# Attention with a token mixer on one core: values on 64 rows of keys, eight tiles and two banks of sums, two banks of scores

## The chip, the cores and the metric

The kernel runs on one core of one Trainium2 chip. Its metric is the device time of one execution in microseconds (us). TensorE (PE) multiplies, VectorE (DVE), ScalarE (ACT) and GpSimd (POOL) do the rest, SyncE (SP) issues most DMAs. PE's results go to PSUM, which has eight banks of 128 x 512 float32; DVE and ACT read them there.

## The reference

`x` is 2048 x 512, `xn` its layer norm. Two branches start from `xn`, and their product is added to `x`:

```
qkv = xn @ wqkv                      # 32 heads of 16
p   = softmax(q @ k.T / 4)           # per head, 2048 x 2048
s   = (p @ v) @ wo
h   = layernorm(xn)
u   = gelu(h.T @ w1 + b1)            # over tokens: 512 x 1792
g   = silu((u @ w2 + b2).T)          # 2048 x 512
out = x + s * g
```

## The kernel before

**Stages.** First come the layer norms and the projections: q and k are written to DRAM in two float32r parts (upper and lower), v as it is. Then a long loop does the attention and, between its matmuls, the mixer branch. At the end the output projection is completed.

**The long loop.** Two heads make a pair; there are 16 pairs. The variable `s` goes by twos. For each pair there is a pass of maxima (`max_of`, line 387: q rows against keys, and on VectorE a maximum of each row, line 391, tile `mxp`) and, `LEAD` = 20 units later, a pass of scores (`score`, line 757, tile `sc`) whose exponentials ScalarE writes to `prob` (line 762). `values` (line 773) multiplies `prob` by `vp`, which holds the values of the pair with a column of ones for the denominator, and sums over the 16 blocks of 128 keys into the bank `av`. A call of `values` is four matmuls, one for each head of the pair and half of the queries; each has all 128 rows of the array and 32 columns, at the output partitions 32j to 32j + 31. They are float32, and each gives two weight loads and two matmuls in the profile. There are 512 calls. After 16 of them `put_away` (line 509) copies the bank to SBUF with ScalarE and sends it to DRAM; for the last pair `own` keeps it on the chip.

**Halves.** Maxima and scores contract over 48 and 50 rows. The heads of a pair sit in partitions 0 to 63 and 64 to 127, so a matmul of one head uses one half of the array's rows, and two matmuls, one in each half, run side by side. The mixer's matmuls (fillers, "D", line 911 after `halves`, tile `dn`) are cut into two of 64 rows for the same reason.

**Order.** The kernel schedules by hand: every engine gets its instructions in the order of the Python code. Within a step of two units, `ORDERS` says which kinds stand in which slot, for the two halves: `s` a score, `m` a maximum, `D` a filler. For six fillers:

```
6: ("DDDDDDsmsmsmsm", "msmsmsmsDDDDDD", 7),
```

`values` of one unit is called ahead of the slot with the number at the end (7), and of the other unit at the end of the step. `run_later` runs what was put off with `after` and `later`.

**Banks of PSUM.** A tile of a pool waits until the last reader of the tile that had its bank is done:

```
ps_sc = pool("ps_sc", 3, space=PSUM)
ps_mx = pool("ps_mx", 3, space=PSUM)
ps_av = pool("ps_av", 1, space=PSUM)
ps_dn = pool("ps_dn", 1, space=PSUM)
```

`ps_sc` holds scores, `ps_mx` maxima, `ps_av` the sums of the values, `ps_dn` those of the mixer and of the output projection. In the projections `bank()` deals out all eight in turn. For `s` below 20, maxima of the second half use `ps_sc` too. From `s` = 512 on there are no more maxima, and the scores of the second half use `ps_mx`. At that time `take` puts whole 128-row fillers (line 886) behind the values.

Of the kernel before, what the change touches and what calls it, by code (L numbers as in the profile page):

```python
# [8 lines left out]
F32 = mybir.dt.float32  # L9
F32R = mybir.dt.float32r  # L10
AF = mybir.ActivationFunctionType
OP = mybir.AluOpType
AX = mybir.AxisListType
PSUM = bass.MemoryType.PSUM
# [7 lines left out]
def tile_attention_token_mixer(ctx, tc, x, wqkv, wo, w1, b1, w2, b2, out):  # L22
    nc = tc.nc
    P = 128
# [5 lines left out]
    NB = S // P  # L30
    ND = D // P
# [9 lines left out]
    def pool(name, bufs, **kw):  # L41
        return ctx.enter_context(tc.tile_pool(name=name, bufs=bufs, **kw))
# [3 lines left out]
    big = pool("big", 4)  # L46
    wp = pool("wp", 4)
    dram = pool("dram", 1, space=DRAM)
    ps_sc = pool("ps_sc", 3, space=PSUM)
    ps_mx = pool("ps_mx", 3, space=PSUM)  # L50
    ps_av = pool("ps_av", 1, space=PSUM)
    ps_dn = pool("ps_dn", 1, space=PSUM)
    ctx.enter_context(tc.manual_schedule())

# [20 lines left out]
    def sub(eng, o, a, b):  # L75
        eng.tensor_tensor(out=o, in0=a, in1=b.bitcast(F32), op=OP.subtract)  # L76

    def move(dst, src, queue=nc.sync):

        queue.dma_start(dst.bitcast(F32), src.bitcast(F32))  # L80
# [7 lines left out]
    qs, ks, vps = {}, {}, {}  # L88
# [62 lines left out]
    with (  # L151
# [26 lines left out]
        for part in range(3):  # L178
            for kd in range(ND):
                nm = ("raw", "wh", "wl")[(part * ND + kd) % 3]  # L180
# [69 lines left out]
        def bank():  # L250

            i = turn_of[0] = (turn_of[0] + 1) % 8
            pl, nm = ((ps_sc, "sc"), (ps_mx, "mx"), (ps_dn, "dn"), (ps_av, "av"))[i % 2 if i < 6 else i - 4]
            return pl.tile([P, 512], F32, name=nm)

        for f in first(0).pieces():
# [14 lines left out]
        for c in range(NC):  # L271
# [23 lines left out]
            for n, (part, g) in enumerate(order):  # L295
                m = slice(g * P, (g + 1) * P)
                ps = bank()
                for w, z in ((wh, 0), (wh, 1), (wl, 0)):
                    for kd in range(ND):
                        nc.tensor.matmul(  # L300
                            ps, w[part][:, kd, m], xt[kd][:, z, :],
                            start=w is wh and z == 0 and kd == 0, stop=w is wl and kd == ND - 1,
# [63 lines left out]
    def after(n, f):  # L366

        later.append(f if n == 1 else lambda: after(n - 1, f))
# [140 lines left out]
    def put_away(p, span, av):  # L509

        ev = el.tile([P, 512], F32, name="ev")
        nc.scalar.copy(ev, av)
        if p == NP - 1:
            own(span, ev)
            return
        g, i = divmod(p, 4)
        if i == 0:
            dens[span] = sm.tile([P, 64], F32, name="d")
        rows = ev.rearrange("(j r) q -> r j q", r=32)
        for a in range(2):  # L520
            h = 2 * i + a
            nc.sync.dma_start(
                dens[span][DH * h : DH * (h + 1), :],
                rows[16 - 16 * a, 2 * a : 2 * a + 2, :].rearrange("c (j q) -> c j q", q=64),
            )
        nc.sync.dma_start(num_d[g][span][160 * i : 160 * i + P, :], ev)
        if i == 3 or p == NP - 2:
            invert(g, span)

    def heads_of(g):  # L530

        return 8 if g < ND - 1 else 6

    def invert(g, span):

        n = heads_of(g)
        d = dens[span][: DH * n, :]

        def two():
            nc.vector.reciprocal(d, d)  # L540
            nc.sync.dma_start(rec_d[g][span][:n, :].rearrange("h (j q) -> (h j) q", j=16), d)
            away.add((g, span))

        after(8 if g < ND - 1 else 4, two)
# [3 lines left out]
    divided = set()  # L548
# [52 lines left out]


    asides = []
    own_done = [False]

    def own(span, ev):
        rq = sm.tile([P, 4, 4], F32, name="rq", bufs=1)
        wide = el.tile([P, 512], F32, name="t", bufs=4)

        def one(pl=ps_mx, nm="mx"):  # L610

            ps = pl.tile([P, 512], F32, name=nm)
            for k in range(4):
                at = slice(k * P, (k + 1) * P)
                nc.tensor.transpose(ps[:, at], ev[:, at], ident)
            turned = ps.rearrange("p (k j r) -> p k j r", k=4, j=4)
            for a in range(2):
                nc.vector.reciprocal(rq[:, :, 2 * a : 2 * a + 2], turned[:, :, 2 * a : 2 * a + 2, 16 - 16 * a])
            nc.vector.tensor_copy(
                wide.rearrange("p (k j r) -> p k j r", k=4, j=4), rq.unsqueeze(3).to_broadcast([P, 4, 4, 32]),  # L620
            )

        def two(pl=ps_mx, nm="mx"):

            ps = pl.tile([P, 512], F32, name=nm)
            for k in range(4):
                nc.tensor.matmul(
                    ps[:, k * P : (k + 1) * P], wide[:, k * P : (k + 1) * P], ident, start=True, stop=True,
                )
            return ps  # L630

        def chunk(ps, of, at):
            nc.vector.tensor_tensor(out=ev[:, at], in0=ps[:, at], in1=ev[:, at], op=OP.mult)
            nc.scalar.copy(of[:, 0, at], ev[:, at])
            sub(nc.vector, of[:, 1, at], ev[:, at], of[:, 0, at])

        if span == QH - 1:
            asides.extend((one, two, chunk))
            return

        def move_in():
            ps = two()
            of = el.tile([P, 2, 512], F32R, name="uo")
            chunk(ps, of, slice(0, 512))
            for a in range(2):
                for c in range(2):
                    row = 32 * (2 * a + c) + DH * a
                    move(oc[ND - 1, c][96 + DH * a : 112 + DH * a, :, :], of[row : row + DH, :, :], nc.gpsimd)
            own_done[0] = True

        asides.extend((one, move_in))


# [93 lines left out]
    state = {}  # L747
    prob = {}
# [15 lines left out]
    def values(t):  # L764
        p, r = divmod(t, SPP)
        span, kb = divmod(r, NB)
        if kb == 0:
            state["av"] = ps_av.tile([P, 512], F32, name="av")
        av = state["av"]
        for a in range(2):  # L770
            for c in range(2):
                j = 2 * a + c
                nc.tensor.matmul(  # L773
                    av[32 * j : 32 * j + 32, :],
                    vps[p][:, kb, 16 * a : 16 * a + 32], prob.pop((t, a, c)),
                    start=kb == 0, stop=kb == NB - 1,
                )
        if kb == NB - 1:
            later.append(lambda: put_away(p, span, av))

    def rest():

        for n in range(N_W - 2, N_W):
            w_split(n)
        for b in range(2):
            load_part(b)

        def until(ready):
            while not ready():
                yield None  # L790

        def products(ps, b, groups, rows=None):
            at = slice(b % 4 * P, (b % 4 + 1) * P)
            for g in groups:
                o = oc[g, b // 4]
                at_g = rows if g == ND - 1 else None
                for j, (m, w) in enumerate(((0, whs), (0, wls), (1, whs))):
                    w = w[N_MIX + g].rearrange("p a b -> p (a b)")
                    yield (
                        ps, lambda r, o=o, m=m, s=at_g: o[s or r, m, at], lambda r, w=w, s=at_g: w[s or r, :],  # L800
                        g == groups[0] and j == 0, g == groups[-1] and j == 2,
                    )

        for b in range(PARTS):
            yield from until(lambda: all((g, b // (NB // QH)) in divided for g in range(ND - 1)))
            ps = ps_dn.tile([P, 512], F32, name="dn")[:, :D]
            yield from products(ps, b, range(ND - 1))
            yield lambda b=b, ps=ps: part(b, ps)
            yield None
        load_last_w()  # L810
        yield from until(lambda: now[0] >= NU and (ND - 1, QH - 1) in divided)
        for n in range(4):
            load_out(n)
        for n, b in enumerate(blocks):
            if n == NB // 2:
                yield from until(lambda: own_done[0] and (ND - 1, 0) in divided)
            ps = ps_dn.tile([P, 512], F32, name="dn")[:, :D]
            rows = slice(0, DH * heads_of(ND - 1) if n < NB // 2 else P)
            if b >= PARTS:
                yield from products(ps, b, range(ND), rows)  # L820
            else:
                yield from products(ps, b, [ND - 1], rows)
            yield lambda n=n, ps=ps: finish(n, ps)
            yield None

    def everything():
        yield from mixer()
        yield from rest()
# [115 lines left out]
    for s in range(0, total + 1, 2):  # L944
        t = s - LEAD
# [79 lines left out]
        if 0 <= t < NT:  # L1025
            p, r = divmod(t, SPP)
# [18 lines left out]
        take(3, lambda x, f: left.append(f) if f else whole(x, f))  # L1045
    for f in left:
        f()
    banks = [(ps_sc, "sc"), (ps_mx, "mx"), (ps_sc, "sc"), (ps_mx, "mx"), (ps_sc, "sc"), (ps_av, "av"), (ps_mx, "mx"), (ps_dn, "dn")]
    half = [NB // 2 + 4 * c + k for k in range(4) for c in range(2)]
    for n, b in enumerate(half):  # L1050
        pl, nm = banks[n]
# [37 lines left out]
```

## Time and profile before

| | us |
|---|---|
| median of 3 runs | 1708.33 (1707.89 to 1708.73) |
| the profiled execution | 1709.11 |
| its span | 1707.3 |
| PE busy | 1672.8 (98%) |
| DVE busy | 1409.7 (83%) |
| ACT busy | 1187.9 (70%) |
| POOL busy | 567.1 (33%) |

The span is the time from the first to the last instruction of that execution. Lines of the page read: line of the kernel, engine, operation, output <- input, shapes and count, then busy time in us and the mean of one in ns, then idle time of the engine just before them and what ended it. "PEld" is a weight load. Shapes such as `128*32` are rows x columns of the array that a matmul uses. In the timeline the columns are start and length in us. The granted clock of TensorE was 0.995 of full speed over the span. The first maximum starts at 153 us, the first score at 207 us, the last maximum at 1613 us and the last score at 1685 us.

### The profile page before, as it was taken

How to read it: one execution, taken by the hardware profiler on the slowest of the kernel's cores; microseconds unless marked ns; L12 is line 12 of the kernel's file. 1: busy time of each engine (PE TensorE's matmuls, PEld its weight loads, DVE VectorE, ACT ScalarE, POOL GpSimd, SP SyncE). 2: the span in 40 equal slices, each digit the busy share in tenths (PEclk: the TensorE clock that was granted, in tenths of full speed). 3: DMA queues.
4: the chain of work that ended last, by engine and by line, in shares of the span. 5: the costliest groups of instructions: out<-in, count | busy, mean ns of one | idle time of the engine just before them, and what ended most of it. 6: DMA issues, size and time to landing. Idle time of an engine off the chain costs nothing.

```text
span 1707.3 us, 30652 instructions
## 1 busy us (share of the span) xinstructions
PE 1672.8 (98%) x11716; PEld 846.9 (50%) x11716; DVE 1409.7 (83%) x2378; ACT 1187.9 (70%) x2291; POOL 567.1 (33%) x673
## 2 busy tenths in 40 slices
PE   7999999999999999999999999999999999999987
PEld 6887644444444444444444444444444444444443
DVE  6565888888888888888888888888888888888834
ACT  3333277777777777777777777777777777787845
POOL 4223842233342334333422322222222222463401
PEclk9999999999999999999999999999999999999999
DMA  6467611415150514353332415141515132272435
GB/s 222 179 235 184 133 44 42 75 44 85 45 85 20 92 46 68 135 127 94 75 60 64 79 35 82 36 80 31 81 33 82 37 48 52 78 158 85 147 98 186
DMA packets 150879, 152.94 MB, mean 90 GB/s; under 512 B 51452, under 2 KB 109820, under 8 KB 147660
## 3 DMA queue, kind: packets, MB, share of 16 engines
q1 hardware_dynamic: 146188, 149.97, 36.8%
q0 software_dynamic: 4544, 1.01, 0.4%
q8 instruction: 92, 1.51, 0.4%
q14 instruction: 55, 0.45, 0.1%
HBM read 100.29 MB, written 49.53 MB: 88 GB/s over the span
## 4 chain that ended last, share of the span: by engine, by line
PE 92%; DVE 5%; ACT 1%; DMA 0%; issue 0%; POOL 0%; SPq 0%; DVEq 0%; POOLq 0%
PE av L773 28%; PE dn L911 26%; PE mx L387 13%; PE sc L757 12%; DVE mxp L391 4%; PE dn L886 3%; PE mx L300 2%; PE sc L300 2%; ACT prob L762 1%; PE av L886 1%; PE av L300 1%; PE dn L300 1%; PE mx L757 1%; PE mx L402 0%; PE sc L83 0%
## 5 line engine op out<-in xcount | busy, mean ns | idle before, releaser
L391 DVE TENSOR_REDUCE mxp<-mx 128x1 f32<-128x512 f32 x2008 | 1250.5, 683 | 183.9 <-PE mx L387 97.4
L762 ACT ACTIVATE prob<-sc 128x512 f32<-128x512 f32 x2008 | 1041.8, 604 | 331.1 <-PE sc L757 252.6
L387 PE MATMUL mx<-big 48*128 48x512 f32 x2008 | 826.8, 428 | 2.1
L757 PE MATMUL sc<-big 50*128 50x512 f32 x2008 | 771.8, 428 | 3.4 <-DMA big<-m 2.0
L911 PE MATMUL dn<-hu,wh 64*128 64x512 f32 x1570 | 573.8, 406 | 0.0
L773 PE MATMUL av<-prob,vp 128*32 128x512 f32 x4096 | 546.3, 605 | 0.0
L387 PEld LDWEIGHTS mx<-big 48*128 48x128 f32 x2008 | 364.2, 186 | 221.8 <-DVE mxp L391 206.6
L757 PEld LDWEIGHTS sc<-big 50*128 50x128 f32 x2008 | 355.1, 185 | 191.7 <-ACT prob L762 173.3
L911 PEld LDWEIGHTS dn<-hu,wh 64*128 64x128 f32 x1570 | 289.3, 185 | 171.5 <-issue 145.5
L911 PE MATMUL dn<-hu,wl 64*128 64x512 f32 x786 | 316.3, 402 | 0.0
L145 POOL CAST wh<-raw 128x512 fp32r<-128x512 f32 x108 | 62.8, 582 | 327.3 <-PE dn L911 309.6
L76 POOL TENSOR_TENSOR wl<-raw,wh 128x512 fp32r<-128x512 f32 x124 | 150.3, 1215 | 38.6 <-ACT wh L147 29.9
L773 PEld LDWEIGHTS av<-prob,vp 128*32 128x32 f32 x4096 | 81.0, 108 | 150.6 <-issue 138.6
L911 PEld LDWEIGHTS dn<-hu,wl 64*128 64x128 f32 x786 | 145.9, 186 | 8.3 <-issue 0.8
L406 POOL CAST m<-f 16x128 fp32r<-16x128 f32 x32 | 9.0, 280 | 266.1 <-DVE f L405 266.1
L464 POOL TENSOR_TENSOR sq<-u 128x512 f32<-128x512 f32 x14 | 14.6, 1040 | 170.9 <-ACT u L463 170.9
L80 POOL DMA_DIRECT2D big<-m x128 | 67.7, 535 | 0.0
L762 ACT ACTIVATE prob<-mx 128x512 f32<-128x512 f32 x40 | 25.1, 627 | 29.2 <-PE sc L757 22.0
L500 POOL TENSOR_SCALAR t<-t 128x512 f32<-128x512 f32 x16 | 23.8, 1488 | 62.4 <-ACT t L497 62.4
L911 PE MATMUL dn<-wh,hu 64*128 64x512 f32 x120 | 41.6, 399 | 0.0
L76 POOL TENSOR_TENSOR hu<-hx,hu 128x512 fp32r<-128x512 f32 x16 | 20.4, 1291 | 54.6 <-ACT hu L243 54.6
L300 PE MATMUL mx<-xt,big 128*128 128x512 f32 x144 | 35.4, 395 | 0.0
(202 smaller groups left out, 1094.2 us busy)
## 6 DMA issues: line engine op xcount, KB each, us to landing
raw<-in_B_w_dram SPq DMA_DIRECT2D x104, 256.0 KB
big<-k_d SPq DMA_DIRECT2D x96, 128.0 KB
big<-q_d SPq DMA_DIRECT2D x96, 128.0 KB
q_d<-sg SPq DMA_DIRECT2D x16, 512.0 KB
k_d<-sg SPq DMA_DIRECT2D x16, 512.0 KB
num_d<-ev SPq DMA_DIRECT2D x30, 256.0 KB
u_d<-uo SPq DMA_DIRECT2D x14, 512.0 KB
hu<-u_d SPq DMA_DIRECT2D x14, 512.0 KB
```

The costliest lines, as they stand in the source:

```text
L76: eng.tensor_tensor(out=o, in0=a, in1=b.bitcast(F32), op=OP.subtract)
L80: queue.dma_start(dst.bitcast(F32), src.bitcast(F32))
L145: nc.gpsimd.tensor_copy(whs[n][:, :m, :], raws[n][:, :m, :])
L300: nc.tensor.matmul(ps, w[part][:, kd, m], xt[kd][:, z, :], start=w is wh and z == 0 and kd == 0, stop=w is wl and kd == ND - 1,)
L387: nc.tensor.matmul(ps, q[o : o + 48, r * P : (r + 1) * P], k[o : o + 48, c * 512 : (c + 1) * 512], start=True, stop=True,)
L391: nc.vector.tensor_reduce(mxp[u // 16][:, a, r % 8, c : c + 1], ps, axis=AX.X, op=OP.max)
L500: nc.gpsimd.tensor_scalar(t, t, 1.0, None, op0=OP.add)
L757: nc.tensor.matmul(ps, ks[p][o : o + 50, kb * P : (kb + 1) * P], qs[p][o : o + 50, at : at + 512], start=True, stop=True,)
L762: nc.scalar.activation(e, ps, AF.Exp, scale=scale)
L773: nc.tensor.matmul(av[32 * j : 32 * j + 32, :], vps[p][:, kb, 16 * a : 16 * a + 32], prob.pop((t, a, c)), start=kb == 0, stop=kb == NB - 1,)
L886: nc.tensor.matmul(ps, w(slice(0, P)), m(slice(0, P)), start=first, stop=last)
L911: made.append(lambda r=r, start=first and a == lead, stop=last and a != lead: nc.tensor.matmul(ps, w(r), m(r), start=start, stop=stop,))
```

## The change

- `values` makes eight matmuls of 64 rows of keys by 32 columns in place of four of 128 rows by 32 columns. Rows 0 to 63 sum into one bank, rows 64 to 127 into a second one.
- `put_away` copies the first bank with ScalarE and adds the second to it with VectorE.
- `ps_av` gets two banks, and `ps_sc` two in place of three.
- The turns of `bank()` and the list of output banks at the end follow the new numbers of banks. `own_done` is set two runs of `run_later` later.

```diff
-    ps_sc = pool("ps_sc", 3, space=PSUM)
+    ps_sc = pool("ps_sc", 2, space=PSUM)
     ps_mx = pool("ps_mx", 3, space=PSUM)
-    ps_av = pool("ps_av", 1, space=PSUM)
+    ps_av = pool("ps_av", 2, space=PSUM)
...
-            pl, nm = ((ps_sc, "sc"), (ps_mx, "mx"), (ps_dn, "dn"), (ps_av, "av"))[i % 2 if i < 6 else i - 4]
+            pl, nm = ((ps_sc, "sc"), (ps_mx, "mx"), (ps_av, "av"), (ps_dn, "dn"))[(0, 1, 2, 1, 0, 1, 2, 3)[i]]
...
         ev = el.tile([P, 512], F32, name="ev")
-        nc.scalar.copy(ev, av)
+        nc.scalar.copy(ev, av[0])
+        nc.vector.tensor_tensor(out=ev, in0=av[1], in1=ev, op=OP.add)
...
-    own_done = [False]
+    own_done = []
...
-            own_done[0] = True
+            after(2, lambda: own_done.append(True))
...
-            state["av"] = ps_av.tile([P, 512], F32, name="av")
+            state["av"] = [ps_av.tile([P, 512], F32, name="av") for _ in range(2)]
         av = state["av"]
         for a in range(2):
             for c in range(2):
                 j = 2 * a + c
-                nc.tensor.matmul(
-                    av[32 * j : 32 * j + 32, :],
-                    vps[p][:, kb, 16 * a : 16 * a + 32], prob.pop((t, a, c)),
-                    start=kb == 0, stop=kb == NB - 1,
-                )
+                e = prob.pop((t, a, c))
+                for half in range(2):
+                    rows = slice(64 * half, 64 * half + 64)
+                    nc.tensor.matmul(
+                        av[half][32 * j : 32 * j + 32, :],
+                        vps[p][rows, kb, 16 * a : 16 * a + 32], e[rows, :],
+                        start=kb == 0, stop=kb == NB - 1,
+                    )
...
-                yield from until(lambda: own_done[0] and (ND - 1, 0) in divided)
+                yield from until(lambda: own_done and (ND - 1, 0) in divided)
...
-    banks = [(ps_sc, "sc"), (ps_mx, "mx"), (ps_sc, "sc"), (ps_mx, "mx"), (ps_sc, "sc"), (ps_av, "av"), (ps_mx, "mx"), (ps_dn, "dn")]
+    banks = [(ps_sc, "sc"), (ps_mx, "mx"), (ps_sc, "sc"), (ps_mx, "mx"), (ps_av, "av"), (ps_av, "av"), (ps_mx, "mx"), (ps_dn, "dn")]
```

## The prediction

> **What bounds the kernel now.** The page comes first. Its parts 1 and 5 say that TensorE is never off for long, and which matmuls fill it:
>
> ```profile
> PE 1672.8 (98%) x11716; PEld 846.9 (50%) x11716; DVE 1409.7 (83%) x2378; ACT 1187.9 (70%) x2291; POOL 567.1 (33%) x673
> ...
> L762 ACT ACTIVATE prob<-sc 128x512 f32<-128x512 f32 x2008 | 1041.8, 604 | 331.1 <-PE sc L757 252.6
> ...
> L773 PE MATMUL av<-prob,vp 128*32 128x512 f32 x4096 | 546.3, 605 | 0.0
> ```
>
> The value products (line 773) have 4096 records, eight to a call, so 512 calls at 546.3 / 512 = 1.07 us. A busy PE hides its stalls, since a matmul's end is modelled. The weight loads show them, so the list of waits is next:
>
> ```profile
> PEld mx L387 <- DVE mxp L391: 206.6, 300, 0.8
> PEld sc L757 <- ACT prob L762: 173.3, 495, 1.1
> ```
>
> Already with three banks of scores a score's weight load is held 495 times until ScalarE has emptied a bank. How such a wait sits in a step is seen in the timeline of one step of two rows of scores (PE, then the loads, then ScalarE: one exponential alone, and the four from the same start merged):
>
> ```profile
> 705.99 1.07 PE L773 MATMUL av<-prob,vp 128*32 128x512 f32 x8
> ...
> 708.54 0.40 PE L387 MATMUL mx<-big 48*128 48x512 f32 x1
> 708.87 1.06 PE L773 MATMUL av<-prob,vp 128*32 128x512 f32 x8
> 709.87 0.49 PE L911 MATMUL dn<-hu,wh 64*128 64x512 f32 x1
> 709.87 0.49 PE L387 MATMUL mx<-big 48*128 48x512 f32 x1
> 710.20 0.39 PE L911 MATMUL dn<-hu,wl 64*128 64x512 f32 x1
> 710.21 0.40 PE L757 MATMUL sc<-big 50*128 50x512 f32 x1
> 710.43 0.39 PE L911 MATMUL dn<-hu,wh 64*128 64x512 f32 x1
> ```
>
> ```profile
> 705.56 0.18 PEld L757 LDWEIGHTS sc<-big 50*128 50x128 f32 x1 [0.20 <-ACT prob L762]
> ...
> 711.74 0.16 PEld L773 LDWEIGHTS av<-prob,vp 128*32 128x32 f32 x8 [0.24 <-issue]
> ```
>
> ```profile
> 704.91 0.60 ACT L762 ACTIVATE prob<-sc 128x512 f32<-128x512 f32 x1 [0.94 <-PE sc L757]
> ...
> 704.91 2.06 ACT L762 ACTIVATE prob<-sc 128x512 f32<-128x512 f32 x4 [0.94 <-PE sc L757]
> ```
>
> What to read. Two matmuls, one in each half of the rows, make a slot of 0.23 us (710.20 to 710.43). Between two calls of the values lie seven slots, and a step is two such windows: from the values at 705.99 to those at 711.74, 5.75 us. A call stretches its place: from the last slot before it (708.54) to the next pair (709.87) are 1.33 us, and that pair then runs 0.49 in place of 0.39 because its weights were not loaded ahead, 0.10 more. So last slot to effective next slot is 1.43, and a window is 7 x 0.23 + 1.43 - 0.23 = 2.81.
>
> A bank of scores is taken for a cycle that the lines give piece by piece. The matmul runs 0.40; ScalarE starts 0.06 later (a score that began at 704.45 ends at 704.85, its exponential starts at 704.91); this takes 0.60; the waiting load begins 0.05 after it (705.51 to 705.56); the load costs 0.10. Sum 1.21 us. ScalarE works faster than that when it has a queue: four in 2.06, so (2.06 - 0.60) / 3 = 0.49 apart.
>
> By the order in the code (the six-filler row of ORDERS), counting slots of a window from 0, the scores stand in slots 1, 3, 5, 6 ahead of the middle values and in 0, 1, 3, 5 behind them. Three banks: in the first window the score of slot 6 (1.38) needs the bank of slot 1 (0.23 + 1.21 = 1.44), 0.06 late; in the second the score of slot 5 (1.15) needs that of slot 0 (1.21), 0.06 late. Step: 2 x 2.81 + 0.12 = 5.74 against 5.75 in the trace. The reading holds, and it can be done again with two banks.
>
> **The change part by part.**
>
> *Two banks of scores.* First window: scores at 0.23 and 0.69; the third (1.15) waits for the first's bank until 1.44, 0.29 late. The second's exponential starts at max(0.69 + 0.46, 0.69 + 0.49) = 1.18 and ends at 1.78, so its bank serves the fourth at 1.93 in place of 1.67, 0.26 more. Together 0.55, against 0.06 now. While the values run, ScalarE empties both banks. Second window: scores at 0 and 0.23; the third (0.69) waits until 1.21, 0.52 late; the second's exponential runs 0.95 to 1.55, bank at 1.70, 0.03 more. Together 0.55 against 0.06. TensorE takes its matmuls in order, so what stands behind the held score (the maxima for VectorE and the fillers of the other half) is held too, and nothing covers it. Per step 2 x 0.49 = 0.98. There are 246 steps that hold both maxima and scores (s from 20 to 510, by twos). 246 x 0.98 = 241 us. If the release were 20% quicker or slower than these rows, 190 to 290.
>
> *Ten steps of the tail* put half the scores on these banks, three in adjacent slots ahead of the values: the third waits from 0.46 to 1.21, 0.75. Some 8 us.
>
> *The first twenty rows of maxima* use the score banks for half of their maxima: five banks in place of six, beside a VectorE that is busy 9.88 of 10.00 us there. TensorE only queues deeper. I take 4, between 0 and 10.
>
> *Values in eight tiles.* The work per row of the array is unchanged: twice the instructions, each on half the rows, all eight at once. The nearest row for halves is the slot itself, whose two 64-row matmuls start within 0.01 us (710.20, 710.21); that for narrow tiles is the present call, whose eight loads take 0.16 us where one takes 0.108, so (0.16 - 0.108) / 7 = 7 ns from one to the next. Four more loads ahead of the last first pass: 4 x 7 = 28 ns, x 512 = 14 us. The bounds are -164 us (all 0.32 of the stretch of a call, 1.43 - 0.23 - 0.88, gone; 0.88 is a call's own streaming, two passes, the second of which starts 0.45 behind the first, at 706.44, and streams 0.43) and +450 (halves one after the other, 0.88 x 512). I take +14, since all rows around are slots in which halves run together. The Trainium skill, "TensorE: Matmul & The Clock Gate", Part 3, puts an additional tile at about 4 ns; by that figure the 14 us would be an estimated 8. No run yet shows eight tiles.
>
> *Two banks of sums, added on put_away.* 32 times VectorE gets one more pass over 128x512 from the sum bank, about the 0.68 of a maximum (it starts one per 0.60), after ScalarE's copy (0.59). The next call that needs these banks begins a window later, 2.81 + 0.55 = 3.36 after the last one, which itself takes 1.06: 2.30 are left, and three hand-overs of 0.06, the copy, up to 0.60 of a running maximum and 0.68 make 2.05. Cover gone, it costs up to 32 x 1.3 = 40. VectorE stands idle some 0.4 us in each 2.87 us window, which takes the added pass. I take 4.
>
> *Rotations of banks in the projections, own_done two calls later, last output bank:* eight banks in eight turns before and after; the delay falls once. Nothing.
>
> Sum against the profiled execution's own 1709.1 us (span 1707.3 and 1.8 around it; the median of the runs is 1708.33): 1709.1 + 241 + 8 + 4 + 14 + 4 = 1980.
>
> **The rivals.**
>
> *A. The switch between tile shapes gets cheap, because the array stays at 64 rows.* The rows speak against it. Ahead of the tail's fillers only the width of the tile changes, with 128 rows kept:
>
> ```profile
> 1625.47 1.07 PE L773 MATMUL av<-prob,vp 128*32 128x512 f32 x8
> 1626.47 0.50 PE L886 MATMUL dn<-wh,hu 128*128 128x512 f32 x1
> ...
> 1629.12 0.39 PE L886 MATMUL dn<-wh,hu 96*128 96x512 f32 x1
> 1629.43 0.50 PE L757 MATMUL mx<-big 50*128 50x512 f32 x1
> ```
>
> From the call to the next matmul 1.00 us, as from 708.87 to 709.87 where rows and width both change; and where only the rows change, 0.31 for a slot of 0.23 and an exposed load again. Any change of shape pays. For A: no row has 64 rows by 32 columns. It would take 0.11 ahead of the call and 0.10 behind it away, 0.21 x 512 = 107: 1873 us, and 1816 if the load is hidden as well. The Trainium skill, "TensorEngine Tiling (Array Packing)", Key Properties, says that a change of tiling mode drains TensorE; by that rule A saves nothing, and the tail's rows agree. Chance 14%.
>
> *B. Faster: the values take half the time.* If each half of the rows streamed its own share at double speed and no switch were left, a call would be 0.45 in place of 1.20 beyond its slot: -0.75 x 512 = -384, so 1596. It decides for faster from 271 / 512 = 0.53 us saved per call. Against it: matmuls of 48, 50 and 64 rows hold a slot of 0.23 exactly as those of 128 rows do (1626.81 to 1627.04), so fewer rows buy no speed. Chance 5%.
>
> *C. The halves run one after the other*, +450 on the sum without the 14: 2416. Against it the pairs of each slot. Chance 5%.
>
> *D. The lost bank binds nothing.* Then only the small terms stay: 1709 + 22 to 30, about 1735. Against it the 495 waits with three banks and a reading that gives the step to 0.01 us. Chance 3%.
>
> **How the numbers follow.** Forecast 73%, time 1980. Its own range, from 190 to 290 for the banks and 0 to 40 for the sums, is 1925 to 2060. The range takes in A's 1873: 1860 to 2060, leaving out B, C, D and the far end of A. About 0.2% (3.4 us) is what a measurement of this kernel can tell from no change. Faster is B, 0.05; same 0.01; slower the rest, 0.94.
>
> **What would show it.** Right: the waits of score loads on prob go from 173 to some 400 us; values-to-values windows at 3.36 in place of 2.87 us; a gap of the PE loads ahead of the third score of each window; busy times of DVE and ACT about unchanged, so at lower shares of a longer span; from a call's first load to the next pair still 1.0 us. A would show in that last figure as 0.9 or less, C as 1.9. The forecast is wrong if the waits on prob stay below 250 us, or if a call of the values takes some other time than its 1.07.

## The result, and the profile after

The changed kernel takes 1976.62 us (median; 1976.24 to 1978.02), the kernel before 1708.11 on the same chip: 1.157 times as long, 95% interval 1.1559 to 1.1586, so 268.5 us slower. The forecast was 1980.0, in a range of 1860 to 2060. The profiled execution has a span of 1976.2 us against 1707.3.

The page after, busy times and the groups that answer to those of before:

```profile
PE 1866.8 (94%) x15812; PEld 885.0 (45%) x15812; DVE 1466.1 (74%) x2410; ACT 1245.0 (63%) x2291; POOL 567.3 (29%) x673
...
L763 ACT ACTIVATE prob<-sc 128x512 f32<-128x512 f32 x2008 | 1096.9, 596 | 516.5 <-PE sc L758 374.2
...
L777 PE MATMUL av<-prob,vp 64*32 64x512 f32 x8192 | 557.8, 602 | 0.0
```

The matmuls of the values doubled in number (8192) and grew by 11.5 us in busy time, 546.3 to 557.8. VectorE and ScalarE do nearly the same work in a longer span. The list of waits after (who waited for whom: us in total, times, the longest):

```profile
PEld sc L758 <- ACT prob L763: 458.3, 1087, 1.5
...
PEld mx L387 <- DVE mxp L391: 151.7, 183, 0.8
...
PE sc L758 <- ACT prob L763: 77.4, 273, 1.1
```

Score loads now wait 1087 times for ScalarE, and 77.4 us of PE itself stand empty for that. One step in the timeline, PE first:

```profile
805.36 1.09 PE L777 MATMUL av<-prob,vp 64*32 64x512 f32 x16
806.38 0.50 PE L915 MATMUL dn<-hu,wh 64*128 64x512 f32 x1
...
807.65 0.39 PE L915 MATMUL dn<-hu,wh 64*128 64x512 f32 x1
807.83 0.98 PE L758 MATMUL sc<-big 50*128 50x512 f32 x2
808.32 0.50 PE L387 MATMUL mx<-big 48*128 48x512 f32 x1
808.75 1.09 PE L777 MATMUL av<-prob,vp 64*32 64x512 f32 x16
809.77 0.49 PE L387 MATMUL mx<-big 48*128 48x512 f32 x1
...
810.98 0.49 PE L758 MATMUL sc<-big 50*128 50x512 f32 x1 [0.25 <-ACT prob L763]
...
812.13 1.09 PE L777 MATMUL av<-prob,vp 64*32 64x512 f32 x16
```

and the weight loads of the same step that were held:

```profile
807.83 0.18 PEld L758 LDWEIGHTS sc<-big 50*128 50x128 f32 x1 [0.22 <-ACT prob L763]
808.32 0.18 PEld L758 LDWEIGHTS sc<-big 50*128 50x128 f32 x1 [0.30 <-ACT prob L763]
...
810.98 0.18 PEld L758 LDWEIGHTS sc<-big 50*128 50x128 f32 x1 [0.68 <-ACT prob L763]
```

From 805.36 to 812.13 the step takes 6.77 us, where 5.75 stood before. The third score of the first window loads at 807.83 and is effective (begins in earnest, once its weights are in) 0.10 later, 807.93, in a slot due at 807.65: 0.28 late, and 0.29 was worked out. The fourth is effective at 808.42 and due at 807.93 + 0.23: 0.26 late, as worked out. In the second window (values at 808.75, next pair at 809.77, effective 809.87) the third score is due at 809.87 + 3 x 0.23 = 810.56 and effective at 811.08: 0.52 late, as worked out. From the call to the next pair are 1.02 us where 1.00 stood before, so the switch between tile shapes costs what it did, within 0.02 us.

The difference of the spans by stages, from the starts of the first and the 481st call of the values in both traces:

| | before | after | more |
|---|---|---|---|
| to the first call | 214.5 | 228.6 | 14.1 |
| first to 481st call | 1374.6 | 1620.0 | 245.4 |
| 481st call to the end | 118.2 | 127.6 | 9.4 |

### The profile page after: what moved, and what is told of

The parts are those of the page before. It is cut to its first block, busy times and chain, and to the rows that moved or that the text cites. A ratio compares the mean times of both kernels' runs of the same rounds, so it can differ in the third digit from the quotient of the medians.

```text
span 1976.2 us, 38913 instructions
## 1 busy us (share of the span) xinstructions
PE 1866.8 (94%) x15812; PEld 885.0 (45%) x15812; DVE 1466.1 (74%) x2410; ACT 1245.0 (63%) x2291; POOL 567.3 (29%) x673
## 4 chain that ended last, share of the span: by engine, by line
PE 87%; ACT 9%; DVE 1%; issue 1%; DMA 0%; POOL 0%; SPq 0%; DVEq 0%; ACTq 0%
PE av L777 26%; PE sc L758 23%; PE dn L915 16%; PE mx L387 11%; ACT prob L763 9%; PE dn L890 3%; PE mx L300 2%; PE sc L300 1%; PE av L300 1%; DVE mxp L391 1%; PE av L890 1%; PE mx L758 1%; PE dn L300 1%; PE sc L387 0%; PE mx L402 0%
## 5 line engine op out<-in xcount | busy, mean ns | idle before, releaser
L391 DVE TENSOR_REDUCE mxp<-mx 128x1 f32<-128x512 f32 x2008 | 1287.8, 686 | 363.4 <-PE mx L387 135.9
L763 ACT ACTIVATE prob<-sc 128x512 f32<-128x512 f32 x2008 | 1096.9, 596 | 516.5 <-PE sc L758 374.2
L758 PE MATMUL sc<-big 50*128 50x512 f32 x2008 | 867.5, 454 | 78.1 <-ACT prob L763 77.4
L915 PE MATMUL dn<-hu,wh 64*128 64x512 f32 x1570 | 596.3, 420 | 0.0
L758 PEld LDWEIGHTS sc<-big 50*128 50x128 f32 x2008 | 352.5, 184 | 470.2 <-ACT prob L763 458.3
L777 PE MATMUL av<-prob,vp 64*32 64x512 f32 x8192 | 557.8, 602 | 0.0
L387 PEld LDWEIGHTS mx<-big 48*128 48x128 f32 x2008 | 356.0, 186 | 189.9 <-DVE mxp L391 151.7
L915 PEld LDWEIGHTS dn<-hu,wh 64*128 64x128 f32 x1570 | 278.2, 185 | 158.4 <-issue 139.5
L777 PEld LDWEIGHTS av<-prob,vp 64*32 64x32 f32 x8192 | 93.0, 104 | 146.2 <-issue 135.3
L915 PE MATMUL dn<-wh,hu 64*128 64x512 f32 x120 | 48.6, 420 | 0.0
L513 DVE TENSOR_TENSOR ev<-av,ev 128x512 f32<-128x512 f32 x32 | 22.1, 692 | 32.0 <-ACT ev L512 27.5
```

Of the source, the lines that this page charges most:

```text
L387: nc.tensor.matmul(ps, q[o : o + 48, r * P : (r + 1) * P], k[o : o + 48, c * 512 : (c + 1) * 512], start=True, stop=True,)
L391: nc.vector.tensor_reduce(mxp[u // 16][:, a, r % 8, c : c + 1], ps, axis=AX.X, op=OP.max)
L758: nc.tensor.matmul(ps, ks[p][o : o + 50, kb * P : (kb + 1) * P], qs[p][o : o + 50, at : at + 512], start=True, stop=True,)
L763: nc.scalar.activation(e, ps, AF.Exp, scale=scale)
L777: nc.tensor.matmul(av[half][32 * j : 32 * j + 32, :], vps[p][rows, kb, 16 * a : 16 * a + 32], e[rows, :], start=kb == 0, stop=kb == NB - 1,)
L915: made.append(lambda r=r, start=first and a == lead, stop=last and a != lead: nc.tensor.matmul(ps, w(r), m(r), start=start, stop=stop,))
```

## The experiments

**The lost bank alone.** The kernel before with one edit to its pools; the projection's turns of banks follow it.

```diff
-    ps_sc = pool("ps_sc", 3, space=PSUM)
+    ps_sc = pool("ps_sc", 2, space=PSUM)
```

> The kernel before with two banks of scores in place of three and nothing else (the turns of the projection's banks go by seven; one PSUM bank stays unused). Bank theory (a bank of scores is taken for 1.21 us, and with two of them a window of seven slots waits 0.55 in place of 0.06 us): nearly all of the loss is here, 1950 to 1970 us, windows between calls of the values 3.36 us, call to next pair 1.00. Shape theory (the eight tiles, their doubled instructions and the added sums cost the time): within 20 us of the time before, 1708 to 1730, windows 2.88.

Measured 1964.85 us against 1708.97, ratio 1.150 (1.1483 to 1.1517): 255.9 of the 268.5 us. The median window between calls is 3.365 us (2.879 before, 3.387 in the changed kernel), and the waits are those of the changed kernel:

```profile
PEld sc L757 <- ACT prob L762: 459.4, 1090, 1.5
...
PE sc L757 <- ACT prob L762: 76.7, 273, 1.1
```

The lost bank makes the loss without any of the rest. From the first to the 481st call this kernel takes 1601.7 us and the changed one 1620.0: the tiles and the added sums cost 18.3 us there, which the next experiment takes apart.

**The tiles' shape taken back.** The calls take the two banks of sums in turn, so each bank gets its last product one call apart from the other.

```diff
-                for half in range(2):
-                    rows = slice(64 * half, 64 * half + 64)
-                    nc.tensor.matmul(
-                        av[half][32 * j : 32 * j + 32, :],
...
+                nc.tensor.matmul(
+                    av[kb % 2][32 * j : 32 * j + 32, :],
+                    vps[p][:, kb, 16 * a : 16 * a + 32], prob.pop((t, a, c)),
+                    start=kb < 2, stop=kb >= NB - 2,
+                )
```

> The changed kernel with the values as four matmuls of 128 rows again, the calls taking the two banks of sums in turn, so that only the shape of the tiles goes back. Bank theory: 12 us off the changed kernel, from the 0.02 us that a call's first load to the next pair grew by (1.019 against 0.996), x 512: 1960 to 1968. Shape theory: most of the 268 us come back, under 1750. If eight tiles had saved part of a switch, it would be slower than the changed kernel.

Measured 1957.71 us (ratio 1.1462, 1.1443 to 1.1482). That is 18.9 below the changed kernel, more than the 9 to 17 expected. The call is back at 0.996 us to the next pair, which is 0.023 x 512 = 12. The rest sits in one window of sixteen, that at the change of a span, where the sums are put away: 3.36 us here, 3.57 in the changed kernel (medians), 32 x 0.2 = 6. That is not the shape but the turns: the bank that ScalarE copies is complete a call earlier here, and VectorE's addition waits for the copy 8.7 us in all, against 27.5 in the changed kernel. The last experiment tests this cause. No part of a switch was saved by tiles of 64 rows.

**The same work in another order.** Two banks of scores, eight tiles, but no two scores in adjacent slots:

```diff
-        6: ("DDDDDDsmsmsmsm", "msmsmsmsDDDDDD", 7),
+        6: ("DDDDDDmsmsmsms", "smsmsmsmDDDDDD", 7),
```

> The changed kernel with another order of the same work in steps of six fillers: scores in slots 0, 2, 4, 6 of each window and maxima in 1, 3, 5, 6 (0, 1, 3, 5 in the second), so that two scores never stand in adjacent slots. Banks, tiles and instructions are the same. Bank theory: the third score waits 1.21 - 0.92 = 0.29 and the fourth 0.03, so 0.32 per window in place of 0.55: windows 3.15 in place of 3.39 us, and 75 to 115 us less in all (not all steps have six fillers), 1860 to 1900. A theory by which the total work of ScalarE or the doubled instructions set the time: no change, 1970 to 1980.

Measured 1893.0 us (ratio 1.1081, 1.1064 to 1.1098), 83.6 less than the changed kernel, with a median window of 3.126 us against the 3.15 expected. Engines, instructions and banks being the same, neither ScalarE's total work nor the doubled instructions can be what sets the time; it is how close the scores stand to each other in TensorE's order. The list of waits is a trap here:

```profile
PEld sc L758 <- ACT prob L763: 501.7, 1088, 1.5
```

It shows more waiting (501.7 against 458.3) in a kernel that is faster. After a call of the values the loads stand 0.84 us whatever comes next, and that is booked on what the first load behind it waits for; in this order the first load is more often a score (284 of the calls against 106). PE's own waits for `prob` fall from 77.4 to 32.9 us.

**The same order with three banks**, the kernel before with that one line changed:

> The kernel before, three banks of scores, with the order that keeps scores apart and puts the maxima in slots 1, 3, 5, 6. Bank theory: no score waits any more (0.06 per window less), but a maximum's bank is taken for 0.40 + 0.06 + 0.68 + 0.05 + 0.10 = 1.29 us, and the fourth maximum (slot 6, 1.38) needs the bank of slot 1 (0.23 + 1.29 = 1.52), 0.14 late: windows 2.88 + 0.08 = 2.96, some 25 to 40 us slower than before, 1733 to 1748. So the same edit that helps with two banks hurts with three. A theory by which this order is better in itself: faster than 1708 by as much as it gains with two banks.

Measured 1744.65 us against 1708.69 (ratio 1.0215, 1.0198 to 1.0232), window 2.97 us: slower by 36.0, as the cycle of a maximum's bank gives it. The list of waits agrees: a maximum's load is held 482 times for VectorE, 300 times before. Here an order is good for its numbers of banks, not in itself.

**The bank taken from the maxima instead**, with eight tiles:

```diff
-    ps_sc = pool("ps_sc", 2, space=PSUM)
-    ps_mx = pool("ps_mx", 3, space=PSUM)
+    ps_sc = pool("ps_sc", 3, space=PSUM)
+    ps_mx = pool("ps_mx", 2, space=PSUM)
```

> The changed kernel with three banks of scores and two of maxima: the bank for the second sum is taken from the maxima. If what counts is a bank in a chain of matmul, reader and release, not scores as such, this loses about as much: third maximum (slot 4, 0.92) waits for 1.29, 0.37 late, the fourth 0.15 more; windows about 3.34 us, 1980 to 2020 in all with the groups of three pairs ahead of the scores short of banks, too. If scores alone are tight: 1720 to 1760.

**and with four tiles and one sum bank**, the kernel before with `ps_mx` at 2:

> The kernel before with two banks of maxima in place of three, one sum bank, four tiles of 128 rows (one PSUM bank unused). Beside the eight tiles with two banks of maxima it gives the price of tiles and sums with three banks of scores: by the longer call, 0.02 x 512 = 12 us, and the added pass on VectorE, now the engine whose release is waited for, 32 x 0.7 = 22: 10 to 35 us less than that kernel. If the tiles' price had been hidden under the waits of scores, the difference would be far larger, over 60 us.

Measured 2011.14 us (ratio 1.1775, 1.1758 to 1.1793) and 1975.82 us (1.157, 1.1549 to 1.1591). In the first, the wait changed its place with the bank:

```profile
PEld mx L387 <- DVE mxp L391: 576.2, 1190, 1.6
...
PEld sc L758 <- ACT prob L763: 78.3, 95, 0.8
```

So it is not the scores as such: whichever of the two chains has only two banks is late. The difference of the two kernels, 35.3 us, is the price of tiles and sums when VectorE's release is what is waited for; it lies just above the 10 to 35 expected. Most of it is at the change of a span, where the added pass stands ahead of the maxima: that window takes 4.16 us in the first kernel and 3.33 in the second.

**The stretch ahead of the scores.**

```diff
-    EARLY = 11
+    EARLY = 7
...
-                if len(first_maxima) == 3 or i == 3 and (s % 16 == 14 or s + 2 == LEAD):
+                if len(first_maxima) == 2 or i == 3 and (s % 16 == 14 or s + 2 == LEAD):
```

> The changed kernel with the maxima ahead of the first scores in groups of two pairs and seven fillers, in place of three pairs and eleven fillers, so that a group needs two banks of each kind. Theory: the first call of the values came 14 us later than before because the third pair of a group waited for a score bank that VectorE still read, with all fillers behind it; here this wait is gone, the first call comes 8 to 15 us earlier than in the changed kernel, and the whole is 1962 to 1970 us. Rival (VectorE is the bound in that stretch, and the 14 us have another cause): first call unchanged at 228 to 230 us, 1974 to 1978 in all.

Measured 1967.69 us (ratio 1.1517, 1.15 to 1.1535); the first call comes at 213.7 us in place of 228.6. What it removes, in the timeline of the changed kernel (PE):

```profile
159.57 0.39 PE L387 MATMUL mx<-big 48*128 48x512 f32 x1
160.87 0.50 PE L387 MATMUL sc<-big 48*128 48x512 f32 x1 [0.91 <-DVE mxp L391]
161.30 0.50 PE L890 MATMUL dn<-hu,wl 128*128 128x512 f32 x1
```

The third pair of a group should start both its matmuls together. With two banks the second of them comes 1.30 us after the first, and the eleven fillers, which need no bank of scores, stand behind it. Of the 14.9 us that the first call is earlier, 10.5 are left in the span: from the 481st call to the end the kernel takes 131.2 us in place of 127.6. More fillers are left for that stretch (147 of their matmuls in place of 125), since a pair of maxima now takes 3.5 along where it took 3.7, and the granted clock falls at other places in it; what each of the two takes stays open.

**The addition of the sums.**

```diff
-        nc.vector.tensor_tensor(out=ev, in0=av[1], in1=ev, op=OP.add)
+        other = el.tile([P, 512], F32, name="other", bufs=1)
+        nc.vector.tensor_copy(other, av[1])
+        nc.gpsimd.tensor_tensor(out=ev, in0=other, in1=ev, op=OP.add)
```

> The changed kernel with the second sum bank copied out by VectorE, and the addition done by GpSimd in SBUF. In the changed kernel the window at the change of a span is 3.55 us, and 3.36 us with 128-row values that take the same two banks and the same addition; and VectorE stands idle 27.5 us (26 times) ahead of the addition until ScalarE's copy is done, with the maxima of the step queued behind it. Queue theory: without the wait for ScalarE the window at the change of span falls to about 3.4, and 32 x 0.15 to 0.2 = 5 to 6 us come back, 1970 to 1972. Rival (the eight tiles cost more there by themselves, by waiting for their two banks): no change, 1976 to 1977, and the wait of the call for its bank stays.

The window at the change of a span falls from 3.57 to 3.385 us, and the 481st call comes at 1842.9 in place of 1848.6 us: the 5.7 us were VectorE's wait for ScalarE, with maxima queued behind. But the whole stays at 1976.52 us (ratio 1.1584, 1.1568 to 1.16), not the 1970 to 1972 expected. From the 481st call to the end it takes 135.3 us in place of 127.6. In that stretch GpSimd waits twice for about 30 us ahead of its two additions:

```profile
POOL ev L515 <- ACT ev L512: 31.8, 1, 31.8
POOL ev L515 <- DVE other L514: 28.4, 1, 28.4
```

These waits explain little of it: TensorE waits for GpSimd's sums 3.7 us there, against 1.5 for VectorE's in the changed kernel. The granted clock of TensorE explains far more. In the rows of the two stretches (start and end; length; busy time and count of PE, PEld, DVE, ACT and POOL; granted clock; DMA share; GB/s) it is 0.96 in the changed kernel, 0.90 here, and 0.59 for 20 us of it:

```profile
1848.60:1976.20 127.60, 108.06 (x839) 51.17 (x838) 63.75 (x108) 67.43 (x131) 20.44 (x26) 0.96 0.41 132
```

```profile
1842.90:1978.20 135.30, 114.78 (x840) 53.44 (x838) 63.20 (x107) 67.56 (x131) 22.98 (x28) 0.90 0.38 124
1904.00:1924.00 20.00, 17.54 (x87) 7.52 (x86) 6.53 (x12) 7.79 (x15) 1.27 (x1) 0.59 0.24 84
```

The same matmuls keep PE busy 6.7 us longer. The whole loss lies between the 496th and the 500th call, 23.5 us in place of 15.7, where the clock was down and a call of the values took 1.96 us. So the gain is there in the loop, and the profiled execution loses it again at a lower clock; whether that clock comes with this kernel or by chance is not shown. Over the span, its five executions have granted clocks of 0.992 to 0.997, the four of the changed kernel 0.996 to 0.998. At 0.997 one of each takes 1974.26 and 1976.45 us, so the expected 5 to 6 us are not seen in the whole there either.

## Why the prediction was right, point by point

- *The bank's cycle.* Worked out 0.98 us more per step; the bank alone gives 2 x (3.365 - 2.879) = 0.97. The single delays agree to 0.01 us. From first to 481st call the terms asked for 240 x 0.98 = 235 for the bank alone, and that kernel takes 227.1 more; some windows carry less than six fillers or the turn of the maxima, and wait less than the reckoned ones (2.74 to 3.12 us in windows of four fillers). That the total is met within 4 us is in part luck: this term is 8 too large, and that of the first twenty rows 10 too small.
- *The call in eight tiles.* Worked out 14 us, measured 0.023 x 512 = 12; 0.023 / 4 is 6 ns for each of the four tiles more, where 7 was read from the row. The Trainium skill's figure of about 4 ns for an additional tile ("TensorE: Matmul & The Clock Gate", Part 3) gave an estimated 8; the measurement lies between the two.
- *The addition on put_away.* 4 us taken, about 6 found, but the reasoning failed: it counted whether the addition is done before the next call. It is. What it passed over is the queue: the addition stands ahead of the step's maxima on VectorE and waits there for ScalarE's copy, 27.5 us of idle time in 26 waits:

```profile
L513 DVE TENSOR_TENSOR ev<-av,ev x32: 685/692/693, 279.9 to 1956.2; 128x512 f32<-128x512 f32 x32
...
  ACT ev L512: 27.5, 26
```

- *The first twenty rows of maxima.* 4 taken, 14.1 found; this term was mis-sized. "TensorE only queues deeper" beside a busy VectorE was the step that failed: TensorE's order puts fillers behind the waiting score bank, so VectorE runs dry while they are made up for. There it was busy 9.88 of 10.00 us before, and is busy 7.33 of 10.00 after (180 to 190 us). Groups that need two banks of each kind gave all of it back: their first call is at 213.7 us, 214.5 before.
- *The tail.* 8 taken, and 9.4 more from the 481st call to the end: the agreement is luck. Of the 9.4, 4.9 lie ahead of the 490th call, in steps that still hold maxima and that the 246 steps count already. Behind it the windows with three scores in adjacent slots grow by 0.8 to 1.3 us, where 0.75 was worked out (from 2.79 to 4.01 at the 506th call). The reckoning left out that ScalarE serves two pools there: the exponential of the score in the other pool goes first, and the held score waits 0.49 longer:

```profile
1936.99 0.60 ACT L763 ACTIVATE prob<-mx 128x512 f32<-128x512 f32 x1 [1.19 <-PE sc L758]
1937.48 0.59 ACT L763 ACTIVATE prob<-sc 128x512 f32<-128x512 f32 x1
```

  Against that, a wait of TensorE for a DMA, 5.1 us in the kernel before, is 0.2 after.
- *The waits.* "Some 400" was the forecast for the score loads, 458.3 the result. One sign was set too tight: a call that takes "some other time than its 1.07" takes 1.09, as the prediction's own 28 ns asked.
- *The range.* Its 190 to 290 for the banks is a fifth of the term, not what a quicker or slower release would do: with a cycle a fifth shorter, 0.97 us, the same reckoning gives some 0.30 per window and 150 in all, an estimate.
- *The rivals.* A (a cheap switch at 64 rows) falls: 1.019 us from a call to the next pair, where 0.9 or less was its sign, and taking 128 rows back made the kernel faster. That agrees with the drain at any change of mode that the Trainium skill states ("TensorEngine Tiling (Array Packing)", Key Properties). B and C fall by the call's 1.09 us against 1.07. D falls by the first experiment.

## What to carry to other kernels

Before a PSUM bank is moved from one chain to another, add up the cycle of a bank (matmul, hand-over, reader, release, load) from the timeline and lay it on the order of the matmuls; an average share of the reading engine (70% here) says nothing about a burst. On an engine that takes its work in order, price a new wait by what stands behind it, fillers and maxima here, and not by whether its own result is in time. In this kernel the order that is good for three banks is wrong for two, and the other way round. And a stretch that got longer is compared in its granted clock first: the idle GpSimd of the last experiment looked like a cause and was hardly one.

## What the runs showed of the hardware that was not expected

Little. The eight tiles of 64 rows by 32 columns, which the kernel before does not have, work side by side at once: sixteen weight loads take 0.18 us together where eight took 0.16, and a call 1.09 us where it took 1.07. And the change between 64 rows by 128 columns and 64 rows by 32 columns costs as much, 1.02 us from a call to the next pair, as one in which the rows change too, 1.00. The granted clock behind the 481st call differs between executions: 0.90 to 0.98 in the traces of the changed kernel and its variants. In the 20 us at 0.59 of the last experiment a call of the values took 1.96 us (the one at 1913.91), and behind them 1.09 again (at 1924.63).
